# Float64 weight correction moved from VectorE to GpSimd, two early loads issued by ScalarE, and a new written order

## The chip, the cores and the metric

One core of one Trainium2 chip runs the whole program. The metric is device time in microseconds (us), the median of three runs. One more run was taken with the hardware profiler; its own time and its span are given below. TensorE (PE) does matmuls and its weight loads (PEld), VectorE is DVE, ScalarE is ACT, GpSimd is POOL, and SyncE (SP) issues DMAs.

## The reference

Attention with 8 batches, 8 heads, 576 positions and head size 64, in which every query keeps only its 32 highest scores, and behind it a SoLU block on 4608 tokens:

```
scores = q @ k.T / sqrt(64)
kth    = the 32nd largest score of each row
attn   = softmax(scores where scores >= kth) @ v
x      = attn as (4608, 512)
h      = x @ w_in                       # w_in (512, 1024), float64
solu   = h * softmax(h)
ln     = (solu - mean) / sqrt(var + 1e-6) * g_ln
out    = ln @ w_out                     # w_out (1024, 512), float64
```

q, k, v and g_ln are float32; w_in and w_out arrive as float64 and are carried as 64-bit words.

## The kernel before

The work is cut into 32 steps (four a batch). A step takes four chunks of 128 queries, two heads each, and one tail chunk, so it has nine blocks of 128 rows by 576 scores, numbered j = 0 to 8. For each step:

- `scores` (L1869) makes the scores on PE in seven units, `evac` (L1892) copies each to the tile X on ACT.
- `estimate`, `length`, `root`, `gained` (L1815 to L1853) work out a first threshold per row; `root` and `gained` are small GpSimd operations.
- `count0` (L1920) counts the scores over it, per block j, on DVE for the first blocks (line L1907) and on ACT for the last three or four (L1915). `second`, `moved`, `even` (L1923 to L1938) form a better threshold, `count1` (L1947) counts again on ACT and leaves the signs in `sg`.
- `side`, `nearest`, `best` (L1955 to L1984) and the steps behind them find the exact 32nd score on DVE from the values nearest to the threshold; `keep` (L2052, line L2055) masks the exponentials E on DVE.
- `transpose_p` and `copy_p` turn E into PT, `attn_v` and `attn_t` multiply it with V on PE, `copy_v` (L2236 to L2249) scales the result on DVE into xTm and xTt. The scales go through DRAM: `turn_r`, `copy_r`, `rd_out`, `rd_in` (L2098 to L2121).

36 blocks of 128 tokens follow as their inputs come ready: `mm1` (L2260), `hexp`, `solu` (L2279), `square`, `spread`, `ln` (L2302, on GpSimd), `transpose_ln`, `copy_ln`, `mm2` (L2324), `store`, `send`.

The weights come in 16 chunks of 128 x 512 64-bit words, in about the first 140 us. For each chunk `load_w` (L1570) brings the raw words, `w_bits` (L1590) forms a float32 from the high words in two DVE operations (L1594, L1598), and `w_corr` (L1603) forms the correction from the low words in two more: L1606 masks out the power of two, L1610 multiplies the low word, 2^-52 and that power. `w_sum` (L1614) adds value and correction on PE by identity matmuls (L1617, L1618), and `w_copy` (L1622) brings the sum into w_in or w_out on ACT. At the end of the kernel the words are loaded again (`w_again`), and `w_exp` (DVE, L1635) and `w_check` (ACT) check their exponents.

`load_k` (L1664) and `load_t` (L1675) bring a head pair's main keys and its 64-row tails; the tails of all pairs go into one tile, `qk_tails`, so the tails of pair n + 1 may be written only after PE has read those of pair n (`prep_k`, L1736). `key_stats` (L1772) of both head pairs of a step come ahead of its `estimate`.

All engines but SP run in an order written out by hand: `PLACES` (L490) holds one number for each piece of work, `arranged` (L472) sorts by it, and the pieces are emitted in that order. Each engine works its own instructions in that order and waits at each for what it needs; SP's DMA issues follow it too. The numbers have no other effect than this order.

Of the kernel before, what the change touches and what calls it, by code (L numbers as in the profile page):

```python
# [465 lines left out]
WIDE_KINDS = ("w_bits", "w_corr", "w_sum", "w_copy", "w_again", "w_exp", "w_check")  # L466
# [5 lines left out]
def arranged(w_wide):  # L472
# [11 lines left out]
    if not w_wide:  # L484
# [10 lines left out]
    ],  # L495
    "load_t": [
# [3 lines left out]
    ],  # L500
    "load_v": [
# [3 lines left out]
    ],  # L505
    "prep_k": [
# [3 lines left out]
    ],  # L510
    "prep_tc": [
# [3 lines left out]
    ],  # L515
    "prep_kc": [
# [3 lines left out]
    ],  # L520
    "key_square": [
# [3 lines left out]
    ],  # L525
    "tail_square": [
# [3 lines left out]
    ],  # L530
    "key_stats": [
# [3 lines left out]
    ],  # L535
    "load_q": [
# [3 lines left out]
    ],  # L540
    "prep_q": [
# [3 lines left out]
    ],  # L545
    "prep_qc": [
# [3 lines left out]
    ],  # L550
    "query_square": [
# [3 lines left out]
    ],  # L555
    "estimate": [
# [3 lines left out]
    ],  # L560
    "length": [
# [3 lines left out]
    ],  # L565
    "root": [
# [3 lines left out]
    ],  # L570
    "gained": [
# [3 lines left out]
    ],  # L575
    "scores": [
        [11258, 12553, 17516, 19137, 11903, 18161, 7601],
        [34101, 29755, 38452, 39097, 26637, 41622, 27493],
        [60356, 61001, 70269, 68119, 59706, 69587, 55581],
        [99604, 94705, 91454, 100249, 94055, 92764, 86988],  # L580
        [130314, 129600, 144747, 140254, 128950, 139466, 131165],
        [173269, 170744, 166391, 165746, 172587, 164928, 161517],
        [204423, 203718, 194005, 195300, 196330, 194650, 201137],
        [231483, 232773, 232128, 229768, 234330, 230833, 235843],
        [251834, 266825, 267507, 265859, 254298, 265209, 247223],
        [284259, 289097, 283545, 288452, 282895, 284941, 286789],
# [820 lines left out]
def fast_path(  # L1407
# [179 lines left out]
    def words(n, k):  # L1587
        return w_raw[n].bitcast(U32).rearrange("p (f w) -> p f w", w=2)[:, :, k]
# [850 lines left out]
```

## Time and profile before

| what | before |
|---|---|
| median of 3 runs | 1107.89 us (1107.51 to 1108.54) |
| the profiled execution: own time | 1107.34 us |
| the profiled execution: span from first to last instruction | 1105.4 us |
| DVE busy | 1005.6 us, 91% |
| PE busy (its ends are modelled) | 1044.7 us, 95% |
| ACT busy | 999.2 us, 90% |
| POOL busy | 241.0 us, 22% |

The chain of waits follows the work that ended last back to the start; the windows give each engine's busy time in a stretch; the rows of lines give a group's busy time, its mean duration in ns, and how long its engine sat idle before it and for whom. A timeline row is start, duration, engine, line, operation, tiles and count, with the idle time before it in brackets.

### The profile page before, as it was taken

The page shows a single profiled execution, that of the slowest core. Times are in us where ns is not written, and L with a number is a line of the kernel's source. Part 1 is how long each engine was busy: PE and PEld are TensorE (multiplying, and loading weights), DVE is VectorE, ACT ScalarE, POOL GpSimd, SP SyncE. Part 2 cuts the span into 40 slices and gives each one's busy share as a digit, 9 for nine tenths or more (in the row PEclk, how much of TensorE's full clock was granted, in tenths as well). Part 3 has the DMA queues.
Part 4 walks back from the last instruction along what each step waited for, and adds up shares of the span by engine and source line. Part 5 has one row for each costly group of instructions (what it writes and reads, how often), then busy time and mean ns, then how long its engine had stood idle before and what let it go on. Part 6 is the DMA issues. An engine that isn't in the chain of part 4 may idle for free.

```text
span 1105.4 us, 22954 instructions
## 1 busy us (share of the span) xinstructions
PE 1044.7 (95%) x7980; PEld 583.2 (53%) x7980; DVE 1005.6 (91%) x2929; ACT 999.2 (90%) x1976; POOL 241.0 (22%) x401
## 2 busy tenths in 40 slices
PE   5778898999999999999999999999999999999996
PEld 3355454554555555555555556555555555555543
DVE  5999999999999999999999898999999989998720
ACT  7999798999999989999998998999999999999632
POOL 1202221303233112222214013212213122220110
PEclk9679899999999999999999999999999999999998
DMA  8312211121121112121121202210211111123411
GB/s 221 112 44 79 79 42 52 34 55 27 48 63 44 53 34 65 31 55 54 47 61 42 53 22 74 55 34 30 67 53 32 44 33 47 49 76 109 155 40 32
DMA packets 110425, 64.81 MB, mean 59 GB/s; under 512 B 89422, under 2 KB 97883, under 8 KB 110299
## 3 DMA queue, kind: packets, MB, share of 16 engines
q1 hardware_dynamic: 110298, 63.25, 20.5%
q8 instruction: 65, 1.06, 0.4%
q14 instruction: 62, 0.50, 0.1%
HBM read 53.65 MB, written 9.57 MB: 57 GB/s over the span
## 4 chain that ended last, share of the span: by engine, by line
DVE 44%; PE 25%; ACT 19%; issue 4%; DMA 1%; POOL 0%; SPq 0%; DVEq 0%; ACTq 0%
DVE w L1971 10%; DVE w L1982 10%; DVE E L2055 8%; PE o_ps L2324 8%; PE h_ps L2260 7%; DVE junkv L1907 5%; ACT sg L1950 5%; ACT X L1902 4%; PE s_ps L1887 3%; DVE solu L2279 3%; ACT PT L2156 2%; ACT E L2007 2%; PE om L2207 2%; DVE by L1999 2%; PE tp_p L1701 2%
## 5 line engine op out<-in xcount | busy, mean ns | idle before, releaser
L2324 PE MATMUL o_ps<-w_out,lnT 128*128 128x512 f32 x576 | 261.1, 599 | 0.9 <-DVE xTt L2249 0.8
L2260 PE MATMUL h_ps<-w_in,xTm 128*128 128x512 f32 x512 | 230.3, 598 | 3.4 <-DVE xTm L2242 2.9
L1982 DVE MAX8 w<-w 128x8 f32<-128x288 f32 x576 | 224.6, 445 | 0.1
L1950 ACT ACTIVATE sg<-X,t 128x576 int8<-128x576 f32 x256 | 198.2, 790 | 7.6 <-DVE t L1935 6.7
L1971 DVE SCALAR_TENSOR_TENSOR w<-X,al,sg 128x576 f32<-128x576 f32 x256 | 202.9, 814 | 0.5
L2055 DVE SCALAR_TENSOR_TENSOR E<-X,kth,E 128x576 f32<-128x576 f32 x256 | 200.2, 821 | 1.3
L2324 PEld LDWEIGHTS o_ps<-w_out,lnT 128*128 128x128 f32 x576 | 105.2, 190 | 119.0 <-issue 113.4
L1887 PE MATMUL s_ps<-kT,qT 64*128 64x192 f32 (+1 forms) x1024 | 155.2, 437 | 12.4 <-ACT kT L1721 4.9
L1907 DVE TENSOR_SCALAR_CACHE_REDUCE junkv<-X,t 128x576 uint8<-128x576 f32 x188 | 146.0, 805 | 8.1 <-ACT X L1902 7.1
L1902 ACT ACTIVATE X<-s_ps 128x768 f32<-128x768 f32 x192 | 146.0, 837 | 7.2 <-PE s_ps L1887 6.9
L2260 PEld LDWEIGHTS h_ps<-w_in,xTm 128*128 128x128 f32 x512 | 94.1, 190 | 110.4 <-issue 102.2
L2007 ACT ACTIVATE E<-X 128x1152 f32<-128x1152 f32 x128 | 150.7, 1201 | 0.0
L2156 ACT COPY PT<-tp_p 128x1024 f32<-128x1024 f32 x128 | 131.7, 1040 | 11.3 <-PE tp_p L1701 8.9
L2207 PE MATMUL om<-PT,vm 128*64 128x256 f32 (+1 forms) x1024 | 135.6, 410 | 2.6 <-ACT PT L2190 1.5
L1887 PEld LDWEIGHTS s_ps<-kT,qT 64*128 64x128 f32 x1024 | 90.9, 197 | 53.8 <-ACT X L1902 7.0
L1842 POOL TENSOR_TENSOR zs<-zs,phalf 128x9 f32<-128x9 f32 x32 | 63.8, 1994 | 173.0 <-DVE zs L1834 138.5
L1701 PE MATMUL tp_p<-ident,E 64*128 64x64 f32 x2048 | 87.8, 229 | 13.0 <-DVE E L2055 8.0
L2207 PEld LDWEIGHTS om<-PT,vm 128*64 128x64 f32 x1024 | 68.9, 137 | 55.2 <-issue 4.0
L1701 PEld LDWEIGHTS tp_p<-ident,E 64*128 64x128 f32 x2048 | 76.4, 142 | 36.2 <-issue 13.3
L1943 POOL TENSOR_SCALAR tt<-t 128x9 f32<-128x9 f32 x32 | 12.9, 403 | 273.0 <-DVE t L1935 239.8
L2295 POOL TENSOR_SCALAR var<-var 128x1 f32<-128x1 f32 x36 | 11.0, 307 | 225.6 <-ACT e_sb L2289 225.2
L2271 ACT ACTIVATE e_sb<-h_ps 128x1024 f32<-128x1024 f32 x36 | 37.5, 1042 | 21.0 <-PE h_ps L2260 21.0
(150 smaller groups left out, 1567.2 us busy)
## 6 DMA issues: line engine op xcount, KB each, us to landing
km<-in_k_dram SPq DMA_DIRECT2D x32, 256.0 KB
q_sb<-in_q_dram SPq DMA_DIRECT2D x64, 128.0 KB
vm<-in_v_dram SPq DMA_DIRECT2D x32, 256.0 KB
out_dram<-osb SPq DMA_DIRECT2D x32, 256.0 KB
scales<-rows SPq DMA_DIRECT2D x58, 128.0 KB
w_raw<-in_moe_w_in_dram SPq DMA_DIRECT2D x8, 512.0 KB
w_raw<-in_moe_w_out_dram SPq DMA_DIRECT2D x8, 512.0 KB
w_again<-in_moe_w_in_dram SPq DMA_DIRECT2D x8, 512.0 KB
```

The source lines that it names most:

```text
L1701: nc.tensor.transpose(out[:, a, :], part(rows), ident[rows, rows])
L1887: nc.tensor.matmul(out=s[:, n, m * part : (m + 1) * part], lhsT=queries_of(i, t)[hd, :], rhs=kT[hd, k0 : k0 + part], start=True, stop=True,)
L1902: nc.scalar.activation(out=x, in_=s, func=AF.Copy, scale=scale)
L1907: nc.vector.tensor_scalar(out=junk, in0=x_of(i, j), scalar1=st[i][t][:, j : j + 1], scalar2=None, op0=ALU.is_ge, op1=ALU.add, accum_out=co ...
L1950: nc.scalar.activation(out=d["sg", j], in_=x_of(i, j), func=AF.Sign, scale=-(1.0 + 2.0**-23), bias=d["t1"][:, j : j + 1], accum_out=column ...
L1971: nc.vector.scalar_tensor_tensor(out=w, in0=x_of(i, j), scalar=d["al"][:, j : j + 1], in1=d.pop(("sg", j)), op0=ALU.subtract, op1=ALU.mult,)
L1982: nc.vector.max(w8[:, j, 8 * half : 8 * half + 8], w[:, half * SH : (half + 1) * SH])
L2007: nc.scalar.activation(out=d["E", t][:, 0 : x2_of(i, t).shape[1]], in_=x2_of(i, t), func=AF.Exp)
L2055: nc.vector.scalar_tensor_tensor(out=e, in0=x_of(i, j), scalar=d["kth"][:, j : j + 1], in1=e, op0=ALU.is_ge, op1=ALU.mult, accum_out=den_a ...
L2207: nc.tensor.matmul(out=o[h * D : (h + 1) * D, cols], lhsT=vm[:, h, c, :], rhs=pt[:, h * NM + c, :], start=(c == 0), stop=False,)
L2260: nc.tensor.matmul(out=h[:, half, :], lhsT=x[:, c, :], rhs=w_in[:, c, half * 512 : (half + 1) * 512], start=(c == 0), stop=(c == NP - 1),)
L2324: nc.tensor.matmul(out=o, lhsT=d["lnT"][:, c, :], rhs=w_out[:, c, :], start=(c == 0), stop=(c == NF - 1),)
```

## The change

1. The second operation of `w_corr` (L1610, DVE) goes. In its place come two GpSimd operations for each chunk: `w_low` turns the low words into float32, times 2^-52, in place, and `w_prod` multiplies them with the power of two. `w_sum` now follows `w_prod`.
2. The three DMAs of `load_t` for pairs 0 and 1 are issued by ACT; those of the other 30 pairs stay with SP.
3. Every place in `PLACES` is a new number, so the order of all pieces on all engines is another one. No piece other than those of 1 is added or left out.

The core of the diff (the places of the other kinds change in the same way):

```diff
-WIDE_KINDS = ("w_bits", "w_corr", "w_sum", "w_copy", "w_again", "w_exp", "w_check")
+WIDE_KINDS = ("w_bits", "w_corr", "w_low", "w_prod", "w_sum", "w_copy", "w_again", "w_exp", "w_check")
...
     "load_t": [
-        0, 10470, 16060, 26190, 37940, 65560, 72482, 102319, 123769, 206223, 214502, 236530, 245024,
...
+        0, 4608, 15310, 25880, 33290, 67285, 78694, 91724, 101724, 195521, 214555, 219213, 231656,
...
     "w_corr": [
-        8667, 13577, 19167, 25147, 28047, 43000, 51790, 61625, 81592, 84152, 97994, 117104, 112195,
-        124205, 131589, 136794,
+        6862, 14072, 19568, 22993, 30672, 35893, 59932, 64324, 71269, 80062, 90454, 96808, 107484,
+        109456, 123803, 132050,
+    ],
+    "w_low": [
+        7192, 14456, 18783, 24773, 29150, 36223, 57745, 62981, 69080, 79245, 89124, 95021, 105950,
+        114239, 124941, 130783,
+    ],
+    "w_prod": [
+        8047, 16116, 20093, 25628, 32452, 39405, 60457, 65379, 73124, 88114, 91577, 97863, 111601,
+        115706, 126841, 133105,
     ],
...
             op0=ALU.bitwise_and,
         )
-        nc.vector.scalar_tensor_tensor(
-            out=corr, in0=words(n, 0), scalar=2.0**-52, in1=corr, op0=ALU.mult, op1=ALU.mult
-        )
+
+    def w_low(n):
+
+        nc.gpsimd.tensor_scalar(
+            out=words(n, 0).bitcast(F32), in0=words(n, 0), scalar1=2.0**-52, scalar2=1.0,
+            op0=ALU.mult, op1=ALU.mult,
+        )
+
+    def w_prod(n):
+
+        corr = w_tmp[n][:, 1, :]
+        nc.gpsimd.tensor_tensor(out=corr, in0=words(n, 0).bitcast(F32), in1=corr, op=ALU.mult)
...
     def load_t(n):
         b, hp = pairs[n]
         hh = slice(2 * hp, 2 * hp + 2)
+        queue = nc.scalar if n < 2 else nc.sync
         for h in range(2):
             hd = slice(h * ST, (h + 1) * ST)
-            nc.sync.dma_start(out=qk_tails[hd, 0, hd], in_=q[b, 2 * hp + h, SM:S, :])
-        nc.sync.dma_start(
+            queue.dma_start(out=qk_tails[hd, 0, hd], in_=q[b, 2 * hp + h, SM:S, :])
+        queue.dma_start(
```

What the new order holds, counted in the sorted lists: the pieces between one step's `second` and the next one's, for the steps from 17 on.

```
interval ending at second(i), i =   17 18 19 20 21 22 23 24 25 26 27 28 29 30 31
scores units, before                 9  5  7  7  9  8  4  7 12  2  7  7  7  7  7
scores units, after                  7  7  7  7  7  7  7  8  6  7  7  7  7  7  7
transpose_p, before                  5  0  5  6  4  5  2  5  6  0  6  4  4  4  7
transpose_p, after                   4  2  6  4  3  5  4  4  4  4  2  5  4  5  6
keep, before                        11  2 12  9 15  7  2 15 12  0 14  9 13  3 15
keep, after                         10  8 14  8  6 12  5 14  4 10  8  9  9  9 18
```

Up to the interval of step 16 both orders hold seven units in each interval. Before the first `count0` of step 0, DVE has three chunks' `w_bits` and `w_corr` in the order before and two in the order after. On ACT, three `evac`, two `exps` and one `w_copy` that stand ahead of `prep_kc` and `key_square` of pair 1 in the order before stand behind them in the order after. Behind the last `keep` of step 31 stand eight `w_exp` in the order before and five in the order after, and the first half of `mm2` of token block 32 now stands on PE just ahead of `turn_r`; otherwise PE's list from there to the end holds the same pieces.

## Rows read from the trace of the kernel before

**Rows 1.** Page, part 1: busy time of each engine, share of the span, instructions.
```profile
PE 1044.7 (95%) x7980; PEld 583.2 (53%) x7980; DVE 1005.6 (91%) x2929; ACT 999.2 (90%) x1976; POOL 241.0 (22%) x401
```
**Rows 2.** Page, part 4: the chain that ended last, share by engine.
```profile
DVE 44%; PE 25%; ACT 19%; issue 4%; DMA 1%; POOL 0%; SPq 0%; DVEq 0%; ACTq 0%
```
**Rows 3.** Windows: stretch, length, busy us and instructions of PE, PEld, DVE, ACT, POOL.
```profile
0.00:30.00 30.00, 17.37 (x115) 10.38 (x116) 16.76 (x46) 23.15 (x54) 5.33 (x43) 0.91 0.82 214
30.00:200.00 170.00, 144.99 (x1081) 82.05 (x1081) 165.00 (x468) 151.79 (x310) 33.16 (x51) 0.88 0.23 64
200.00:600.00 400.00, 393.90 (x3128) 221.91 (x3130) 394.53 (x1159) 388.85 (x775) 104.28 (x149) 1.00 0.18 47
600.00:700.00 100.00, 99.75 (x827) 57.31 (x824) 91.88 (x272) 94.10 (x180) 20.97 (x34) 1.00 0.21 56
700.00:900.00 200.00, 196.72 (x1551) 110.38 (x1549) 195.13 (x571) 192.32 (x382) 43.98 (x71) 1.00 0.16 43
900.00:1020.00 120.00, 118.11 (x910) 65.32 (x908) 111.28 (x321) 114.56 (x219) 22.98 (x39) 1.00 0.22 67
1020.00:1041.00 21.00, 19.90 (x176) 11.03 (x172) 20.69 (x64) 13.19 (x22) 4.53 (x6) 1.00 0.26 81
1041.00:1105.50 64.50, 54.02 (x226) 24.78 (x222) 10.31 (x37) 21.23 (x41) 5.79 (x9) 0.95 0.21 71
```
**Rows 4.** Waits of DVE from 30 to 1045 us: total us, times, longest.
```profile
DVE al L1959 <- ACT sg L1950: 8.3, 9, 2.6
DVE junkv L1907 <- ACT X L1902: 7.1, 7, 2.3
```
**Rows 5.** Timeline of PE late in the kernel, and its group of lines.
```profile
L2324 PE MATMUL o_ps<-w_out,lnT 128*128 128x512 f32 x576 | 261.1, 599 | 0.9 <-DVE xTt L2249 0.8
...
1070.84 3.60 PE L2324 MATMUL o_ps<-w_out,lnT 128*128 128x512 f32 x8
```
**Rows 6.** Lines of DVE: busy us, mean ns of one, idle before.
```profile
L1610 DVE SCALAR_TENSOR_TENSOR w_tmp<-w_raw,w_tmp 128x512 f32<-128x512 uint32 x16 | 11.1, 693 | 0.5
...
L1635 DVE TENSOR_SCALAR w_exp<-w_again 128x512 uint32<-128x512 uint32 x16 | 6.6, 418 | 0.5 <-DMA w_again<-in_moe_w_out_dram 0.4
```
**Rows 7.** Lines and timeline: GpSimd's ln, alone and beside DVE's L1971.
```profile
L2302 POOL TENSOR_SCALAR solu<-solu,nmu,rstd 128x1024 f32<-128x1024 f32 x36 | 52.6, 1461 | 2.7
...
271.65 2.48 POOL L2302 TENSOR_SCALAR solu<-solu,nmu,rstd 128x1024 f32<-128x1024 f32 x1
...
271.61 1.53 DVE L1971 SCALAR_TENSOR_TENSOR w<-X,al,sg 128x576 f32<-128x576 f32 x2
...
1072.39 1.20 POOL L2302 TENSOR_SCALAR solu<-solu,nmu,rstd 128x1024 f32<-128x1024 f32 x1
```
**Rows 8.** Timeline of the head: tails' loads, first transposes, second statistics, first count.
```profile
1.54 1.32 SPq L1680 DMA_DIRECT2D qk_tails<-in_q_dram  x2
...
4.54 0.88 PE L1701 MATMUL tp_k<-ident,qk_tails 64*128 64x64 f32 x3 [4.54 <-DMA qk_tails<-in_q_dram]
...
7.96 1.14 SPq L1680 DMA_DIRECT2D qk_tails<-in_q_dram  x2
...
17.13 0.17 DVE L1775 TENSOR_TENSOR stats<-sums,heads 128x6 bf16<-128x6 f32 x1 [3.06 <-ACT junka L1760]
...
20.73 0.81 DVE L1907 TENSOR_SCALAR_CACHE_REDUCE junkv<-X,t 128x576 uint8<-128x576 f32 x1
```
**Rows 9.** Timeline of DVE: three of its longer waits after 600 us.
```profile
686.45 0.81 DVE L1907 TENSOR_SCALAR_CACHE_REDUCE junkv<-X,t 128x576 uint8<-128x576 f32 x1 [2.31 <-ACT X L1902]
...
909.90 0.16 DVE L1959 SCALAR_TENSOR_TENSOR al<-n,tt 128x3 f32<-128x3 f32 x1 [2.59 <-ACT sg L1950]
...
1011.83 0.16 DVE L1959 SCALAR_TENSOR_TENSOR al<-n,tt 128x3 f32<-128x3 f32 x1 [2.31 <-ACT sg L1950]
```
**Rows 10.** Timeline of DVE: the last keep, and the first work behind it that waits.
```profile
1040.08 0.81 DVE L2055 SCALAR_TENSOR_TENSOR E<-X,kth,E 128x576 f32<-128x576 f32 x1
...
1052.99 0.42 DVE L2242 TENSOR_TENSOR xTm<-om,scales 128x256 f32<-128x256 f32 x1 [9.44 <-DMA scales<-rows]
```

More of the change, by code (lines that the diff above doesn't have):

```diff
@@ new lines @@
+        [418590, 422749, 424404],
+        [452470, 450937, 445478],
+        [477483, 481195, 482713],
+        [505619, 516227, 511076],
+        [545047, 549481, 536746],
+        [564045, 562089, 557252],
+        [601445, 610894, 606233],
+        [643774, 634569, 637711],
+        [672761, 661316, 667592],
+        [703135, 696636, 700755],
+        [727715, 724003, 731412],
+        [759304, 756889, 765270],
+        [787034, 790733, 783309],
+        [822109, 820397, 814205],
+        [848274, 855359, 840877],
@@ new lines @@
+        [275108, 285359],
+        [305449, 305883],
+        [342206, 347449],
+        [370873, 376052],
+        [390631, 400502],
+        [429461, 422421],
+        [457046, 456922],
+        [483828, 479154],
+        [510983, 526282],
+        [541356, 574329],
+        [581133, 594733],
+        [610272, 622309],
+        [642613, 647265],
+        [669277, 681514],
+        [707340, 712474],
+        [723112, 740238],
+        [763699, 774869],
+        [792960, 799382],
+        [829587, 840506],
@@ L1112 @@
-        [1026055, 1024041],
+        [54788, 56731],
+        [86178, 96392],
+        [132116, 121257],
+        [161139, 153396],
+        [188898, 200924],
+        [227288, 225994],
+        [244648, 242500],
+        [280606, 285906],
+        [308109, 309511],
+        [344219, 350235],
+        [371736, 377034],
+        [393321, 401987],
+        [430842, 423036],
+        [458616, 457306],
+        [485060, 481832],
+        [514166, 526673],
+        [551059, 579023],
+        [581827, 595573],
@@ L1113 @@
+        [612000, 622770],
+        [644939, 648033],
+        [676025, 684516],
+        [709801, 718583],
+        [728282, 741554],
+        [766692, 775349],
+        [795173, 799855],
+        [836821, 841177],
+        [862460, 869152],
+        [893255, 883843],
+        [914013, 925937],
+        [944496, 949092],
+        [973617, 984528],
+        [1003660, 1003226],
     ],
     "attn_v": [
-        [75477, 80408],
-        [102152, 96541],
-        [147218, 152075],
-        [177266, 174067],
@@ new lines @@
+        [379898, 382102],
+        [409138, 411342],
+        [444994, 447198],
+        [467404, 465448],
+        [503773, 501995],
+        [531375, 533579],
+        [574627, 592032],
+        [604720, 606924],
+        [632843, 635047],
+        [660696, 662900],
+        [690830, 689048],
+        [717425, 719629],
+        [744888, 751386],
+        [776098, 778889],
+        [824352, 830630],
+        [854864, 857068],
+        [878348, 880552],
+        [899044, 901248],
+        [926782, 928986],
@@ L1147 @@
+        [961242, 965949],
+        [984112, 987038],
+        [1005787, 1004009],
     ],
     "attn_t": [
[L1149 to L1163 removed]
@@ new lines @@
+        [138041, 145323],
+        [170322, 169895],
+        [222428, 217936],
+        [232966, 232539],
+        [260671, 263036],
+        [290487, 291021],
+        [337677, 338211],
+        [366823, 367357],
+        [383880, 384414],
+        [413594, 414128],
+        [448976, 449510],
+        [470035, 469608],
+        [506404, 505977],
+        [535357, 535891],
+        [576884, 593863],
+        [608702, 609236],
+        [636825, 637359],
+        [665158, 664731],
+        [693461, 693034],
@@ L1209 @@
-        [903052, 902720],
-        [930671, 931133],
-        [957593, 968345],
-        [985616, 986078],
-        [1013854, 1013522],
-        [1034742, 1035204],
+        [65379, 75503],
+        [94826, 101494],
+        [142570, 146360],
+        [171614, 170697],
+        [223558, 218870],
+        [235158, 234726],
+        [262887, 263772],
+        [292157, 291825],
+        [338694, 339156],
+        [368121, 368583],
+        [388723, 389185],
+        [418658, 415298],
+        [450143, 450605],
@@ new lines @@
+        [470871, 470449],
+        [510614, 510282],
+        [536814, 537276],
+        [578410, 595200],
+        [610100, 610562],
+        [637779, 638241],
+        [666270, 665938],
+        [696173, 696704],
+        [722801, 722469],
+        [749605, 756477],
+        [780295, 781497],
+        [827995, 837022],
+        [859791, 860253],
+        [884159, 883100],
+        [903850, 904312],
+        [933822, 948215],
+        [964655, 968525],
+        [989640, 990902],
+        [1011467, 1011929],
@@ L1271 @@
-        [1042750, 1046185],
-        [1050539, 1057409],
+        [105772, 102337],
+        [109314, 113919],
+        [175773, 172338],
+        [184448, 187883],
+        [235882, 239721],
+        [243918, 249835],
+        [293056, 297763],
+        [309622, 306187],
+        [317764, 314329],
+        [376350, 372008],
+        [391496, 385617],
+        [433497, 430062],
+        [437041, 440476],
+        [471675, 484429],
+        [497729, 494294],
+        [541957, 545392],
+        [553232, 549797],
@@ new lines @@
+        [561565, 556776],
+        [611765, 615309],
+        [627716, 624281],
+        [669878, 673313],
+        [681812, 677718],
+        [723713, 727148],
+        [735487, 740529],
+        [782419, 785854],
+        [799673, 793832],
+        [804380, 808928],
+        [862009, 866351],
+        [874191, 870756],
+        [910494, 907059],
+        [931465, 934900],
+        [972852, 969417],
+        [979831, 976396],
+        [1012554, 1015989],
+        [1019531, 1022966],
+        [1027177, 1030612],
@@ L1348 @@
-        [1010972, 1015263],
-        [1018805, 1025501],
-        [1053974, 1061700],
-        [1065242, 1069533],
-        [1073075, 1076617],
+        [131150, 139178],
+        [155067, 159719],
+        [195368, 199703],
+        [203247, 208000],
+        [263630, 268035],
+        [275778, 279322],
+        [321199, 325251],
+        [342807, 347740],
+        [352206, 356611],
+        [396458, 400800],
+        [415331, 418873],
+        [453374, 458150],
+        [475110, 479445],
+        [507105, 511832],
@@ new lines @@
+        [522734, 527572],
+        [565000, 569955],
+        [577585, 582726],
+        [596403, 599947],
+        [638810, 643717],
+        [652756, 656539],
+        [694162, 698876],
+        [708926, 713268],
+        [753811, 757353],
+        [764300, 771321],
+        [812363, 815905],
+        [833416, 836958],
+        [842171, 845715],
+        [890592, 894136],
+        [914899, 921757],
+        [938335, 942980],
+        [950510, 954293],
+        [989944, 993486],
+        [999185, 1009119],
@@ L2386, in fast_path @@
         copy_v, mm1, hexp, solu, square, spread, ln, transpose_ln, copy_ln, mm2, store, send, load_g, turn_g,
-        copy_g, load_w, w_bits, w_corr, w_sum, w_copy, w_gain, w_again, w_exp, w_check, w_passed,
+        copy_g, load_w, w_bits, w_corr, w_low, w_prod, w_sum, w_copy, w_gain, w_again, w_exp, w_check, w_passed,
         w_verdict,
```

728 lines of the change are left out of this document (269 added, 459 removed), and 588 rows, old and new, of the table PLACES.

## Prediction

> **What bounds the kernel now.** I read part 1 of the page first, then the chain, then the windows, then the waits of the engine that the chain names. Part 1 has three engines at 90% or more and GpSimd at 22% [rows 1]; PE looks the fullest. The chain says otherwise: 44% of it is DVE, 25% PE, 19% ACT [rows 2]. The windows say where: DVE sits idle for 13.2 of the first 30 us, then for 5.0 in 30 to 200, 5.5 in 200 to 600, 8.1 in 600 to 700, 4.9 in 700 to 900, 8.7 in 900 to 1020 and 0.3 up to 1041 [rows 3]. So from 30 to 1041 us it works 97% of the time, and its list sets the pace up to the last `keep`, which ends at 1040.9 [rows 10]. What is left of idle time there are mostly waits for ACT: 8.3 us for the signs and 7.1 us for X [rows 4]. Behind the last `keep` comes a tail of 64.5 us, in which DVE has 10.3 us of work and PE 54.0 [rows 3].
>
> PE's 95% is not a bound of the same kind. A 512-column matmul is listed at 599 ns, yet eight in a row take 3.60 us, 0.45 each [rows 5]; the recorded busy time holds overlap and queueing. The Trainium skill, Trainium Kernel Development and Optimization, section Performance Expectations, calls matmul busy time a bad metric because matmuls are pipelined. By that rule the trace agrees, and it lowers the chance of the third rival below.
>
> The end is therefore: DVE's idle time in the head, plus its work up to the last `keep`, plus its waits in the middle, plus the tail. I go through these four, against the profiled execution's own 1107.34 us; 1.9 us of it lie around the span, and the median of the runs stands 0.55 above it.
>
> **DVE's work.** Sixteen L1610 operations of 693 ns go, 11.1 us [rows 6], all in the first 140 us and in a stretch where DVE is 97% busy. Since everything behind stands in DVE's list, all of it moves up: -11.1. The other three operations of a chunk stay. Three more `w_exp` of 418 ns now stand ahead of the last `keep` [rows 6]: +1.3. The two GpSimd operations cost DVE nothing as far as the trace shows: beside a GpSimd operation of 2.48 us two L1971 of 576 columns took 1.53 us [rows 7], no more for a column than L1610's 693 ns for 512 [rows 6].
>
> **The GpSimd operations.** The trace has none of this size. The nearest is `ln`, a one-input operation on 1024 columns: 1.20 us alone, 1.46 on average, 2.48 beside L1971 [rows 7]. For 512 columns `w_low` lies between half the lowest, 0.6, and the highest, 2.48; I take 0.75, near half the mean. `w_prod` reads two tensors; I put it between 0.6 and 2.48 and take 1.2, above half the mean since it reads twice. `w_low` runs beside what is left of `w_corr`, so `w_sum` comes 1.2 - 0.69 = 0.5 us later for each chunk. Behind `w_sum` on PE stand scores and transposes, and behind those `evac` and `count0`. What covers it: PE has 25.0 us idle in 30 to 200 and 12.6 in the first 30 [rows 3], and 16 x 0.5 = 8 us go into that. I charge +0.5; without the cover it would be +8, and at the highest durations it is the last rival. GpSimd itself has room: 16 x 1.95 = 31 us beside 38.5 us that it is busy in the first 200 [rows 3]. `root` now stands behind such pieces in its list; a step's first count could start a us or two late, which I keep in the range.
>
> The trace shows the shared cost in the other direction: the same `ln` takes twice as long beside an operation of DVE that reads two tensors [rows 7]. The Trainium skill, GPSIMD Engine Reference, section 1 (Specifications), says the SBUF interfaces are shared with VectorE, with contention when DVE reads two SBUF inputs; the trace agrees, 1.20 against 2.48 us. Its section 3 (Performance versus the Vector engine) speaks against this change: GpSimd is called the wrong choice for ordinary elementwise work, and a two-input operation is put at about 2.6 cycles an element at 1.2 GHz. From that an estimate for `w_prod` is 1.1 us without start-up; the sum by it would not differ by more than 0.1.
>
> **The head.** SP issues the tails of pair 0 from 1.54 us on and those of pair 1 from 7.96 on [rows 8]; on ACT the second set can go out as soon as PE has read the first, which ends near 4.54 + 0.88 = 5.4, some 2.5 us sooner. The second statistics come at 17.13 and the first count at 20.73 [rows 8]. In the new order ACT also turns to pair 1 before three copies, two `exps` and a `w_copy`, so the first count should start four to five us earlier. But that is not four us of gain: one chunk of some 2.2 us (an estimate: two operations like each of [rows 6], 2 x 0.69 + 2 x 0.42) is done after it instead of before. Up to the count DVE has three chunks of work now, 6.7 us and under 2 us of small pieces, so it idles some 12 of the 20.73 us; with two chunks, and the count near 16, it idles some 11. ACT pays three issues of 0.66 us, half of 1.32 [rows 8], ahead of its first copies. I take -1.0, between -4 (all of the earlier start) and +3 (ACT's wait for PE and its issues delay the first keys, and the count stays where it was).
>
> **The middle.** This is where I chose most. In the even part, 200 to 600 us, DVE idles 1.4 us per 100 [rows 3]. In 600 to 700 and 900 to 1020 it idles 16.8 us in 220, where that rate would give 3.0: an excess of 13.8. The order before is uneven there. Between the `second` of steps 17 and 18 it has five scores units and no transpose, later nine, eight, four, twelve and two units, and from 0 to 15 `keep`; the wait at 686.45 lies in an interval with nine units, that at 909.90 in one with 13 `keep` [rows 9]. The new order has seven units in nearly every interval and 4 to 14 `keep` in those of the same steps. Where ACT is handed its work evenly, I expect the even rate. One place stays uneven: 18 `keep` stand ahead of `second` of the last step (15 before), so I keep the 2.3 us wait at 1011.83, just behind that `second` [rows 9]. That makes -11.5. The bounds are wide: +5 (ACT and PE, which have less room when all else is 20 us shorter, make DVE wait as much as before and a little more) and -20 (nearly all waits go).
>
> **The tail.** The pieces behind the last `keep` are the same, but half a `mm2`, 3.6 us [rows 5], now stands ahead of `turn_r`. It starts while the last `keep` still runs and ends after it; of its length I count 1.5 against the path that goes through the scales' trip to DRAM, which DVE waits 9.44 us for [rows 10]. Fewer `w_exp` behind it change nothing, DVE is idle there. +1.5, between 0 and +3.
>
> **Sum.** -11.1 + 1.3 + 0.5 - 1.0 - 11.5 + 1.5 = -20.3 us, so 1107.34 - 20.3 = 1087.0 for a profiled execution, and 1087.6 for the median.
>
> **Rivals.**
> 1. Only the removed work counts. The waits of the middle stay in size and change place, because ACT, at 90% [rows 1], is as full as before. The waits for ACT speak for it [rows 4]; that they cluster where the order is uneven speaks against it. -20.3 + 11.5 = -8.8: 1099.1.
> 2. More comes: of the 27.2 us idle in 200 to 1020 [rows 3], 15.7 in the forecast, only 10 stay, and the first count keeps more of its lead. -20.3 - 5.7 - 3 = -29.0: 1078.9. For it: 0.3 us idle in 1020 to 1041, so DVE can run without waits. Against it: even the long even part idles 1.4 per 100 us, which is 11 for those 820 us.
> 3. PE is the bound after all and takes back what DVE gives: no change, 1108. For it: 393.9 of 400 us busy [rows 3]. Against it: the 0.45 us above, and a chain with 44% DVE.
> 4. Slower. GpSimd's two operations take 2.48 us each, since DVE reads two tensors for most of the time. Then 4.96 us stand where 0.43 + 0.69 stood, each `w_sum` is 3.8 us late, and what queues behind it on PE with it: 16 x 3.8 = 61 us, of which the 37.6 us of PE's idle time before 200 us take up their part. 61 - 37.6 = 24 late, less the gain of 20.3: 1111. It decides from (37.6 + 20.3) / 16 = 3.6 us a chunk on. Against it: 2.48 is a worst case for twice the columns.
>
> **How the numbers follow.** The forecast 0.55, rivals 1 to 4 with 0.21, 0.11, 0.05 and 0.08. The forecast's own range is 1081 to 1093. To leave out 2 in 10, the range reaches to rival 2 and past rival 1: 1079 to 1101. Within 0.2% (2.2 us, about what a measurement of this kernel tells from no change) is rival 3; slower is rival 4. Faster 0.87, same 0.05, slower 0.08.
>
> **What would show it.** In the changed kernel's windows DVE's busy total is 11 us lower, and the last `keep` ends near 1019. `w_prod` is near 1.2 us, and PE's waits for it at L1617 and L1618 sum to under 8 us. The first count starts near 16 us. DVE's waits for X and the signs fall from 15.4 to about 5 us, with none over 1 us in 600 to 700. From the last `keep` to the end stay 64 to 67 us. The prediction is wrong in its main step if the waits of the middle come back elsewhere (time near 1099), and in its cover if waits for `w_prod` exceed 15 us before 150 us.

## The result, and the profile after

The changed kernel takes 1093.41 us (median of 4 runs, 1092.84 to 1094.46) where the kernel before takes 1108.22 (1107.51 to 1109.45, run beside it): a ratio of 0.9866 with a 95% interval of 0.9849 to 0.9883. It is 14.8 us faster, where 20.3 were forecast; the forecast for the median was 1087.6. The profiled execution has a time of its own of 1093.13 us and a span of 1091.3.

First part 1 and the chain of the page of the kernel after, which answer to [rows 1, 2]:

```profile
PE 1037.9 (95%) x7980; PEld 582.7 (53%) x7980; DVE 1001.0 (92%) x2913; ACT 998.4 (91%) x1976; POOL 284.5 (26%) x433
...
PE 51%; DVE 28%; ACT 15%; issue 3%; DMA 1%; POOL 1%; SPq 0%; DVEq 0%; ACTq 0%
```

Sixteen operations fewer stand on DVE, 11.1 us of work by [rows 6], yet its busy time fell by 4.6 us only. The chain now follows PE for half of its length, as it does for 40 to 53% in every kernel below with the new order and for 23 to 27% in those with the old one. The windows of the kernel after, in the columns of [rows 3], say where the time went:

```profile
0.00:30.00 30.00, 15.86 (x92) 9.33 (x94) 12.85 (x35) 17.91 (x41) 11.38 (x50) 0.97 0.76 189
30.00:200.00 170.00, 143.83 (x1110) 82.83 (x1106) 166.81 (x462) 156.13 (x323) 68.90 (x79) 0.87 0.25 69
200.00:600.00 400.00, 396.36 (x3147) 222.74 (x3147) 395.52 (x1164) 393.57 (x780) 101.33 (x147) 1.00 0.18 48
600.00:700.00 100.00, 99.91 (x834) 57.83 (x831) 95.71 (x281) 95.67 (x186) 21.63 (x35) 1.00 0.20 54
700.00:900.00 200.00, 198.22 (x1563) 112.05 (x1562) 196.96 (x583) 197.36 (x397) 45.22 (x70) 1.00 0.17 45
900.00:1003.00 103.00, 103.00 (x831) 58.43 (x830) 98.82 (x289) 98.45 (x185) 25.50 (x36) 1.00 0.24 76
1003.00:1026.60 23.60, 23.33 (x179) 12.69 (x178) 23.03 (x65) 18.01 (x32) 4.79 (x8) 1.00 0.38 114
1026.60:1091.30 64.70, 57.36 (x241) 26.81 (x241) 11.28 (x41) 21.32 (x39) 5.80 (x9) 0.96 0.17 55
```

The third pair is DVE. It idles 17.15 us of the first 30 (13.2 before), 3.2 up to 200 (5.0), 4.5 up to 600 (5.5), 4.3 in 600 to 700 (8.1), 3.0 up to 900 (4.9) and 4.2 in the 103 us up to 1003. The last `keep` ends at 1028.6 where it ended at 1040.9. I cut both traces at 30 us, at 200 us and at the end of the last `keep`, and count DVE's idle time in each part, its busy time up to the last `keep`, and the rest:

```
                                 before    after   measured   forecast
DVE busy, up to the last keep     995.2    991.7     -3.5       -9.8
DVE idle, 0 to 30                  13.2     17.1     +3.9       -1.0
DVE idle, 30 to 200                 5.0      3.2     -1.8       +0.5
DVE idle, 200 to the last keep     27.5     16.6    -10.9      -11.5
last keep to the end of the span   64.6     62.8     -1.8       +1.5
sum                                                 -14.1      -20.3
```

### The profile page after: what moved, and what is told of

Same layout as the page of the kernel before. It is cut to its first block, busy times and chain, and to the rows that moved or that the text cites. A ratio compares the mean times of both kernels' runs of the same rounds, so it can differ in the third digit from the quotient of the medians.

```text
span 1091.3 us, 22980 instructions
## 1 busy us (share of the span) xinstructions
PE 1037.9 (95%) x7980; PEld 582.7 (53%) x7980; DVE 1001.0 (92%) x2913; ACT 998.4 (91%) x1976; POOL 284.5 (26%) x433
## 4 chain that ended last, share of the span: by engine, by line
PE 51%; DVE 28%; ACT 15%; issue 3%; DMA 1%; POOL 1%; SPq 0%; DVEq 0%; ACTq 0%
PE o_ps L2342 15%; PE h_ps L2278 13%; PE s_ps L1905 6%; DVE w L1989 6%; PE om L2225 6%; DVE w L2000 6%; DVE E L2073 5%; ACT sg L1968 4%; DVE junkv L1925 4%; PE tp_p L1719 4%; ACT X L1920 2%; ACT E L2025 2%; ACT PT L2174 2%; DVE solu L2297 2%; PE s_ps L1894 2%
## 5 line engine op out<-in xcount | busy, mean ns | idle before, releaser
L2073 DVE SCALAR_TENSOR_TENSOR E<-X,kth,E 128x576 f32<-128x576 f32 x256 | 204.0, 829 | 2.0 <-ACT E L2025 1.4
L1989 DVE SCALAR_TENSOR_TENSOR w<-X,al,sg 128x576 f32<-128x576 f32 x256 | 205.1, 824 | 0.1
L1905 PE MATMUL s_ps<-kT,qT 64*128 64x192 f32 (+1 forms) x1024 | 149.5, 430 | 4.3 <-DVE solu L2297 1.7
L1925 DVE TENSOR_SCALAR_CACHE_REDUCE junkv<-X,t 128x576 uint8<-128x576 f32 x188 | 148.5, 804 | 5.1 <-ACT X L1920 4.0
L1860 POOL TENSOR_TENSOR zs<-zs,phalf 128x9 f32<-128x9 f32 x32 | 68.7, 2146 | 161.6 <-DVE zs L1852 148.4
L1961 POOL TENSOR_SCALAR tt<-t 128x9 f32<-128x9 f32 x32 | 16.2, 508 | 250.6 <-DVE t L1953 208.8
L2313 POOL TENSOR_SCALAR var<-var 128x1 f32<-128x1 f32 x36 | 13.9, 387 | 196.7 <-ACT e_sb L2307 196.4
L2320 POOL TENSOR_SCALAR solu<-solu,nmu,rstd 128x1024 f32<-128x1024 f32 x36 | 53.6, 1490 | 3.3
```

The costliest lines, as they stand in the source:

```text
L1905: nc.tensor.matmul(out=s[:, n, m * part : (m + 1) * part], lhsT=queries_of(i, t)[hd, :], rhs=kT[hd, k0 : k0 + part], start=True, stop=True,)
L1925: nc.vector.tensor_scalar(out=junk, in0=x_of(i, j), scalar1=st[i][t][:, j : j + 1], scalar2=None, op0=ALU.is_ge, op1=ALU.add, accum_out=co ...
L1989: nc.vector.scalar_tensor_tensor(out=w, in0=x_of(i, j), scalar=d["al"][:, j : j + 1], in1=d.pop(("sg", j)), op0=ALU.subtract, op1=ALU.mult,)
L2073: nc.vector.scalar_tensor_tensor(out=e, in0=x_of(i, j), scalar=d["kth"][:, j : j + 1], in1=e, op0=ALU.is_ge, op1=ALU.mult, accum_out=den_a ...
```

## The experiments

The medians below are of four to twelve timed runs, but for one kernel with a single run; the ratio is to the kernel before, run beside it on the same chip (medians of 1108.3 to 1109.3 us), with its 95% interval. Kernels that ran on different chips are best compared by these ratios. "Held" is counted in the trace in this way: an operation of DVE that ends over 150 ns later behind its forerunner than the median of its kind does, beside a running GpSimd operation; the excess over the median is the held time. DVE's counts are left out: some of them show 0.16 to 0.18 us also where GpSimd rests.

### What each part of the change is worth

**Order alone.** The changed kernel, with the low words multiplied on DVE again and all tails loaded by SP:

```diff
+        nc.vector.scalar_tensor_tensor(
+            out=corr, in0=words(n, 0), scalar=2.0**-52, in1=corr, op0=ALU.mult, op1=ALU.mult
+        )
...
     def w_low(n):
-        nc.gpsimd.tensor_scalar(...)
+        pass
     def w_prod(n):
-        nc.gpsimd.tensor_tensor(...)
+        pass
...
-        queue = nc.scalar if n < 2 else nc.sync
+        queue = nc.sync
```

> The new order with the old work: the low words are multiplied by VectorE again, in one operation behind the mask at w_corr's places, and all tails are loaded by SyncE at their new places. Theory A (the gain is the order's; the move to GpSimd is worth about nothing because GpSimd's operations hold VectorE's; the loads by ScalarE cost about 4 us in the head): VectorE gets 11.1 us back and loses 10.4 us of holds, the head regains 4: about 1090 us. Theory B (the move is worth its 11 us, and the order lost it elsewhere): 1093.4 + 11 - 4 = about 1100 us. If SyncE's tails of pair 1, which now stand ahead of the second keys, hold back the loads behind them, both are some us later, and the first count shows it.

Measured: 1092.40 us, ratio 0.9848 (0.9835 to 0.986). The order alone makes the whole gain, as theory A had it. The window of this kernel from 200 us on:

```profile
200.00:1020.00 820.00, 813.98 (x6468) 459.67 (x6464) 802.80 (x2357) 799.11 (x1569) 198.33 (x296) 1.00 0.19 53
```

DVE idles 17.2 us from 200 to the last `keep`, as in the kernel after (16.6). Its whole busy time is 1001.5 us with the sixteen operations in it, against 1001.0 in the kernel after without them.

**The move undone, the loads kept on ACT.** The first two hunks of the diff above, without the third.

> The changed kernel with one part undone: the low words are multiplied by VectorE again, in one operation behind the mask, in the new order and with ScalarE's loads of the first tails kept. Theory A (the move to GpSimd is worth about nothing, since holds give back what VectorE saves): 1092 to 1095 us, beside 1093.4 for the changed kernel. Theory B (the move gains at least a few us in the order that was made for it): over 1097 us.

Measured: 1094.14 us, 0.9863 (0.9845 to 0.988); DVE busy 1001.1 us, idle 17.3 us from 200 to the last `keep`. Beside the kernel after (1093.41 us, 0.9866) the move to GpSimd is worth -0.7 us, or +0.3 by the ratios. The kernel with all tails on SP, shown below, gives a second pair that differs in the move alone, both run on the same chip: 1092.96 us with the low words on GpSimd, 1092.40 with them on DVE, +0.6. In the new order the move can't be told from nothing.

**The move alone, in the old order.** The kernel before with `w_low` and `w_prod` on GpSimd, placed right behind their `w_corr`:

```diff
+    "w_low": [8668, 13578, 19168, 25148, ...
+    "w_prod": [8669, 13579, 19169, 25149, ...
...
-        nc.vector.scalar_tensor_tensor(...)
+    def w_low(n):
+        nc.gpsimd.tensor_scalar(...)
+    def w_prod(n):
+        nc.gpsimd.tensor_tensor(...)
```

> The kernel before, its order and its loads, with the low words on GpSimd: w_low and w_prod directly behind w_corr. Theory A (holds give back what VectorE saves): VectorE loses 11.1 us of its own work and gains 8 to 12 us of holds: 1106 to 1109 us. Theory B (the move is worth its 11 us): 1097 to 1099 us. A third reading (TensorE waits for GpSimd at w_sum): over 1110 us.

Measured: 1112.98 us, 1.0034 (1.0023 to 1.0045): some 4 us slower. Its window from 200 us on:

```profile
200.00:1020.00 820.00, 808.01 (x6406) 454.96 (x6405) 792.94 (x2323) 789.72 (x1551) 191.13 (x292) 1.00 0.18 50
```

And two lines of its timeline:

```profile
104.08 2.59 DVE L1982 SCALAR_TENSOR_TENSOR w<-X,al,sg 128x576 f32<-128x576 f32 x2
104.33 1.72 POOL L1623 TENSOR_TENSOR w_tmp<-w_raw,w_tmp 128x512 f32<-128x512 f32 x1 [5.30 <-DVE w_tmp L1608]
```

DVE's idle time from 200 on is 27.5 us, as before: the middle belongs to the order. The pair of `w` operations took 2.59 us beside `w_prod`, 1.53 in [rows 7]. Over the kernel `w_prod` held 12 of DVE's operations for 11.9 us and `w_low` 11 for 4.0: 15.9 us lost against 11.1 saved. The time is that of the third reading, PE waiting for `w_prod`, but the cause is not: PE does wait 6.0 us for it between 20 and 160 us, yet of the 4.9 us that the span is longer, 4.6 are DVE's busy time up to the last `keep`, and its idle time up to 200 us grew by 0.7 only.

**The loads, by themselves.** The changed kernel with the tails of pairs 0 and 1 on SP (third hunk above), and the kernel before with them on ACT (`queue = nc.scalar if n < 2 else nc.sync`, as in the change):

> The changed kernel with the tails of pairs 0 and 1 issued by SyncE again, at the same places; nothing else differs. Theory A (the issue by ScalarE delays the head: the tails land late beside the first weights, and ScalarE's table load waits behind the issues): first count 4 to 5 us sooner than the 21.7 of the changed kernel, about 1089.5 us. Theory B (the head is limited by what lands, whoever issues it): first count within 1 us and 1093 to 1095 us.

> The kernel before with the tails of pairs 0 and 1 issued by ScalarE, at the places before. Theory A (the issue by ScalarE delays ScalarE's first work in any order, but a lead of 3 us in the first count is lost again by 190 us): first ScalarE operation at 10 us or later instead of 5.9, first count 2 to 4 us later than 20.7, and the time the same within 2 us, 1107 to 1111 us. Theory B (the delay in the head is of the new order alone): first count within 1 us of 20.7 and the time that of before.

Measured: 1092.96 us, 0.9852 (0.9839 to 0.9864) with SP; 1109.45 us, 1.0006 (0.9997 to 1.0015) for ACT in the old order. By total time the loads make no difference that can be told: going by the ratios, their issue by ACT costs 1.6 us in the kernel after, 1.7 in the new order with the low words on DVE and 0.7 in the old order, always the same way, but with intervals that overlap. Their delay in the head is real: the first count starts at 18.1 us with SP and 21.7 with ACT in the new order, 20.7 and 23.3 in the old one. Where the new order's SP kernel loses its lead, the windows show; first this kernel, then the kernel after:

```profile
125.00:140.00 15.00, 11.82 (x91) 7.53 (x90) 12.72 (x35) 9.48 (x14) 9.72 (x13) 0.77 0.19 54
...
170.00:190.00 20.00, 20.00 (x168) 11.96 (x165) 17.64 (x53) 15.43 (x23) 0.00 (x0) 0.91 0.16 45
```

```profile
125.00:140.00 15.00, 11.81 (x69) 5.97 (x69) 14.83 (x45) 10.37 (x23) 6.67 (x8) 0.92 0.31 89
...
170.00:190.00 20.00, 20.00 (x194) 12.07 (x192) 20.00 (x59) 16.61 (x27) 1.14 (x2) 1.00 0.17 47
```

The lead of 3.5 us, measured at the `second` of a step, holds until step 3 and is gone at step 5. In these stretches DVE idles 4.6 us where the kernel after idles 0.2, waiting for X, and PE's granted clock is 0.77 and 0.91 on average where the kernel after has 0.92 and 1.00. Whether the clock is the cause was not settled. Over the first 200 us DVE idles the same in both: 14.0 + 6.3 us with SP, 17.1 + 3.2 with ACT.

### What the GpSimd operations cost

**No low words at all.** The changed kernel without `w_low` and `w_prod`, the correction masked to zero (the low words are left out of the weights):

```diff
-            out=corr.bitcast(U32), in0=val.bitcast(U32), scalar1=0xFF800000, scalar2=None,
+            out=corr.bitcast(U32), in0=val.bitcast(U32), scalar1=0x0, scalar2=None,
```

with both bodies replaced by `pass`.

> The changed kernel without w_low and w_prod, and no operation in their place: the correction is masked to zero, so the low words of the weights are left out. Theory A (holds cost VectorE about 10 us on the path): 1093.4 - 10 = about 1083 us, VectorE's held operations before 140 us gone. Theory B (the held time would have been waiting time anyway, VectorE waits for ScalarE or TensorE instead): 1091 to 1094 us.

Measured: 1087.46 us, 0.9806 (0.9792 to 0.982), 5.9 us below the kernel after (6.6 by the ratios), between the two theories. DVE's busy time up to the last `keep` is 981.5 us, 10.1 below, though DVE itself does the very same list. The windows:

```profile
0.00:30.00 30.00, 17.23 (x108) 9.93 (x108) 11.87 (x38) 18.98 (x45) 4.83 (x43) 0.94 0.77 194
30.00:200.00 170.00, 146.32 (x1147) 84.86 (x1146) 163.56 (x474) 159.97 (x329) 37.46 (x56) 0.88 0.24 68
```

GpSimd is down from 68.90 to 37.46 us in 30 to 200, and DVE gets through 474 operations where the kernel after gets through 462. Of the 10.1 us, 4.7 come back as idle time: 1.0 more up to 30 us, 3.3 more in 30 to 200, 0.4 behind.

**The same work in small pieces.** `w_low` in two pieces of 256 columns, `w_prod` in four of 128, so that a hold would be short:

```diff
+        for c in range(4):
+            cols = slice(c * 128, (c + 1) * 128)
+            corr = w_tmp[n][:, 1, cols]
+            nc.gpsimd.tensor_tensor(
+                out=corr, in0=words(n, 0)[:, cols].bitcast(F32), in1=corr, op=ALU.mult
+            )
```

> The changed kernel with w_low cut into two operations of 256 columns and w_prod into four of 128; the arithmetic and the places are the same. Theory A (an operation of VectorE that reads two tensors waits for the end of the GpSimd operation that is running, whatever its length): the held time by w_low and w_prod falls from 10.4 us to 2 to 4, and the time to between that of the run without low words (1087.5) and the changed kernel (1093.4): about 1089 us. Theory B (VectorE is slowed in proportion to GpSimd's work, so every piece holds again): held time stays at 9 to 11 us, 1093 to 1096 us.

Measured: 1091.73 us, 0.9854 (0.9839 to 0.987). DVE busy up to the last `keep` 988.8 us, 2.8 below; the holds of the low words are 28 for 6.5 us, none over 0.31 us, where they were 15 for 10.4. Its line of `w_prod`:

```profile
L1633 POOL TENSOR_TENSOR w_tmp<-w_raw,w_tmp 128x128 f32<-128x128 f32 x64 | 36.5, 601 | 23.4 <-DVE w_tmp L1614 20.9 <-PE tp_k L1725 1.6 <-DVE t L1955 0.7
```

And two pieces of its timeline, the first undisturbed by DVE:

```profile
8.66 1.72 POOL L1633 TENSOR_TENSOR w_tmp<-w_raw,w_tmp 128x128 f32<-128x128 f32 x4 [0.44 <-DVE w_tmp L1614]
...
92.92 3.85 POOL L1633 TENSOR_TENSOR w_tmp<-w_raw,w_tmp 128x128 f32<-128x128 f32 x4
93.57 1.01 DVE L2079 SCALAR_TENSOR_TENSOR E<-X,kth,E 128x576 f32<-128x576 f32 x1
94.50 1.00 DVE L2079 SCALAR_TENSOR_TENSOR E<-X,kth,E 128x576 f32<-128x576 f32 x1
```

In the kernel after, the first `w_prod`, whole and undisturbed as well, is

```profile
8.78 1.29 POOL L1629 TENSOR_TENSOR w_tmp<-w_raw,w_tmp 128x512 f32<-128x512 f32 x1 [1.15 <-DVE w_tmp L1614]
```

Beside the four pieces of 92.92 each `keep` takes 1.0 us where it takes 0.81 undisturbed: the two engines take turns. The price is on GpSimd, 36.5 us where 24.6 were: four pieces take 1.72 us undisturbed where one whole takes 1.29, and the rest is waiting for DVE. The time fell by 1.7 us (1.3 by the ratios), with intervals that overlap.

**`ln` in four pieces**, 256 columns each, in the changed kernel, by the same means.

> The changed kernel with ln, the GpSimd operation on 1024 columns of each token block, cut into four of 256; everything else as changed. It holds VectorE for 8.1 us in 13 places in the changed kernel (4.8 us in 7 places before). Theory A (holds end with the GpSimd operation, and they lie on VectorE's path): held time by ln under 3 us, and 4 to 6 us off: about 1088 us. Theory B (held time is waiting time in any case, or the pieces hold as often): 1092 to 1096 us.

Measured: 1095.69 us, 0.9882 (0.9868 to 0.9896): 2.3 us above the kernel after, as theory B had it. The holds by `ln` fell from 8.0 to about 6 us, but its 144 pieces take

```profile
L2322 POOL TENSOR_SCALAR solu<-solu,nmu,rstd 128x256 f32<-128x256 f32 x144 | 110.8, 781 | 3.2
...
1061.33 2.16 POOL L2322 TENSOR_SCALAR solu<-solu,nmu,rstd 128x256 f32<-128x256 f32 x4
```

110.8 us, where 36 whole ones take 53.6. Undisturbed, at 1061.33, four pieces take 2.16 us where one whole `ln` takes 1.20 [rows 7]: 36 times that difference is 35 of the 57 us, and the rest is waiting. Cutting an operation shortens each hold, but buys it with GpSimd time.

### The head

**Table first.** An activation of one column ahead of ACT's loads, in the changed kernel (a single run):

```diff
+    warm = const.tile([P, 1], F32, tag="warm", name="warm")
+    nc.scalar.activation(out=warm, in_=phalf, func=AF.Exp)
```

> The changed kernel with one small activation of one column ahead of all of ScalarE's work, so that the load of its table, 1.28 us, comes before the issues of the tails and not behind them. Theory A (the table load behind the issues is part of the delay): ScalarE's first copy at about 10 us instead of 11.2, and the first count 1 us sooner than 21.7. Theory B (the late tails alone set it, their landing at 7.0 and 7.8 us): the tails of pair 0 go out 1.2 us later and the first copy comes no sooner than 11.2. The whole time within 2 us of 1093 in both.

Measured: 1091.37 us; the table load starts at 0.72 us, the first copy at 8.57 where it was 11.21, and the first count at 19.9. Its lead over the kernel after, 1.8 us at the `second` of step 0, is still 1.8 at that of step 31. The same edit on the kernel with the low words on DVE, and on the one with small pieces:

> The new order with the low words on VectorE, ScalarE's loads kept, and the early table load: the same test of the head without GpSimd's operations. Theory A (the table's 1.8 us is kept): 1.5 to 2 us below the run with the move undone. Theory B (the lead is lost): the same time as it.

> A version meant to beat the changed kernel: w_low in two and w_prod in four pieces, and the small activation ahead of ScalarE's loads that brings the table load forward. Theory A (both effects are separate: holds of 10.4 us fell to 6.5 for about 1.7 us of time, the earlier table gave 1.8 us): 1089 to 1090.5 us. Theory B (a lead from the head is lost again by 190 us, as with the tails by SyncE): 1091 to 1092 us.

Measured: 1091.93 us, 0.9843 (0.9827 to 0.9858) and 1089.13 us, 0.9825 (0.9806 to 0.9844). Each is 2.0 to 2.6 us below its partner without the edit (1093.41, 1094.14, 1091.73). Where both of a pair have intervals they overlap, and the first was run once, but all three go the same way. The last one, quarters and table, is the fastest kernel that computes the whole reference: its interval lies below that of the changed kernel, 0.9849 to 0.9883.

## Why the prediction came out as it did

**The middle: right in size, and shown to be the order's.** Waits from 200 us on fell by 10.9 us, 11.5 forecast. The three kernels with the old order have 27.4 or 27.5 us there, every kernel with the new one 16.5 to 17.5, whatever multiplies the low words and whoever loads. So the order did it. That its evenness did it is argued and not tested, and the count of units alone doesn't tell where the waits stood: in the trace of before the waits for X and the signs between the `second` of step 16 and that of step 31 sum to 11.9 us, of which 4.9 lie in the four intervals with more than seven units, 6.9 in the eight with just seven and 0.1 in the three with fewer. In the kernel after they sum to 2.0. The waits for the signs and X from 30 to 1030 us, which answer to [rows 4]:

```profile
DVE junkv L1925 <- ACT X L1920: 3.2, 6, 1.3
...
DVE al L1977 <- ACT sg L1968: 2.7, 4, 1.9
```

They sum to 5.9 where about 5 were forecast. The wait that I kept, for the signs just behind the `second` of the last step, is still there, 1.9 us for the 2.3 that were kept:

```profile
997.50 0.16 DVE L1977 SCALAR_TENSOR_TENSOR al<-n,tt 128x3 f32<-128x3 f32 x1 [1.87 <-ACT sg L1968]
```

Rival 1, in which the waits only change place, falls on this, though its 1099 us lay no farther from the result than the forecast. The mark for 600 to 700 held: the one wait of over 1 us that is left there, 1.15 us, is for the exponentials E and not for X or the signs. Rival 2 falls as well, 16.6 us of waits stay where it left 10. Rival 3, PE as the bound that takes everything back, falls by the time; with a chain that now follows PE for half of its length, PE bounds more of the kernel than it did, and by how much no experiment took apart.

**DVE's work: the step that failed.** "The two GpSimd operations cost DVE nothing as far as the trace shows" is wrong. They hold DVE's operations. The clearest place in the timeline of the kernel after:

```profile
27.81 1.56 DVE L1602 TENSOR_SCALAR w_tmp<-w_raw 128x512 uint32<-128x512 uint32 x1
...
27.79 1.29 POOL L1629 TENSOR_TENSOR w_tmp<-w_raw,w_tmp 128x512 f32<-128x512 f32 x1 [2.55 <-DVE t L1949]
```

An operation that takes 0.42 us undisturbed (L1594 of before, the same operation) starts 0.02 us behind `w_prod` and takes 1.56: it ends 0.29 us behind `w_prod`'s end. A little later both directions stand in a row:

```profile
95.63 0.81 DVE L2073 SCALAR_TENSOR_TENSOR E<-X,kth,E 128x576 f32<-128x576 f32 x1
95.73 1.88 POOL L1629 TENSOR_TENSOR w_tmp<-w_raw,w_tmp 128x512 f32<-128x512 f32 x1
96.37 1.85 DVE L2073 SCALAR_TENSOR_TENSOR E<-X,kth,E 128x576 f32<-128x576 f32 x1
97.69 1.04 POOL L1621 TENSOR_SCALAR w_raw<-w_raw 128x512 f32<-128x512 uint32 x1
98.15 1.18 DVE L2073 SCALAR_TENSOR_TENSOR E<-X,kth,E 128x576 f32<-128x576 f32 x1
```

The `keep` of 95.63 was first and keeps its 0.81 us; `w_prod`, 0.10 us behind it, takes 1.88 instead of 1.29; the next `keep` starts while `w_prod` runs and takes 1.85. Here whoever starts first goes on, and the other waits for its end. In [rows 7] stands such a wait too, and I misread it: there two DVE operations in a row, the first 0.04 us ahead of `ln`, were the ones that went on and `ln` waited, and I took DVE to be immune. The trace of before had the other case too, six times, 4.6 us in all, always beside `ln`; here the first:

```profile
128.36 1.86 POOL L2302 TENSOR_SCALAR solu<-solu,nmu,rstd 128x1024 f32<-128x1024 f32 x1
...
129.24 1.58 DVE L2055 SCALAR_TENSOR_TENSOR E<-X,kth,E 128x576 f32<-128x576 f32 x1
```

Three of these six are such operations of `keep`, whose mean of 821 ns over 256 hid them. With `ln` the recorded start does not always decide. Eleven of its 36 operations in the kernel after take 1.87 us or more, and in each of these, as in [rows 7], a two-input operation of DVE that started behind `ln` was not held, so that `ln` waited for it as well. Here the second of the two operations starts 0.58 us behind `ln` and goes ahead of it:

```profile
905.64 2.37 POOL L2320 TENSOR_SCALAR solu<-solu,nmu,rstd 128x1024 f32<-128x1024 f32 x1
...
905.50 1.53 DVE L1989 SCALAR_TENSOR_TENSOR w<-X,al,sg 128x576 f32<-128x576 f32 x2
```

The Trainium skill, SBUF — State Buffer, section SBUF: two separate sides, has the rule: VectorE and GpSimd share a pair of ports as an exclusive lock, held for a whole instruction by whichever of a GpSimd operation and a VectorE operation of certain kinds (two SBUF inputs, or a two-port mode) starts first. By that rule the rows of `w_prod` agree, and the eleven `ln` don't by their recorded starts; why is open. Held in the kernel after were 24 operations with two inputs and four TENSOR_SCALAR, for 1.13 us at most. Whether those four ran in a two-port mode no run shows. None of the 41 MAX8 was held that started with at least 0.3 us of `w_low`, `w_prod` or `ln` still to run.

In the kernel after `w_prod` holds 9 operations for 8.0 us, `w_low` 6 for 2.4, and `ln` 13 for 8.0 (4.6 before). So DVE's busy time of -4.6 us splits as: -11.1 for the operations taken away, +10.4 for the holds by the two new ones, +3.4 for more holds by `ln`, which stands elsewhere in the new order; the remaining -7.3 is what is left over. In the order-only kernel the same comparison (1005.6 to 1001.5 us, 3.0 more held by `ln`) leaves -7.1, so it comes from the order too; it lies in many small operations that follow sooner on their forerunners (the 32 operations that form `zk_all` add 7.5 us to the busy time where they added 8.5). No experiment took that apart. It is also where luck came in: 13.8 us of holds that the forecast did not have were half made up for by 7 us that it did not have either. Taking the low words away altogether gives back 5.9 of the 10.4 us, and the old order, where more operations are caught, turns the move into a loss: both show the holds to be the price.

The other half of the step, that all of the 11.1 us move up, was too high as well. The kernel without low words lies 6.7 us below the one with the sixteen operations back on DVE (1087.46 and 1094.14; 6.3 by the ratios), and DVE idles 5.0 us more in it. So even without any hold the move would have been worth some 6 us in the new order, not 11.

**GpSimd's durations: nearly right, and the wrong question.** Lines of GpSimd in the kernel after:

```profile
L1629 POOL TENSOR_TENSOR w_tmp<-w_raw,w_tmp 128x512 f32<-128x512 f32 x16 | 24.6, 1540 | 32.3 <-DVE w_tmp L1614 24.3 <-PE s_ps L1905 5.0 <-DVE t L1949 2.6
L1621 POOL TENSOR_SCALAR w_raw<-w_raw 128x512 f32<-128x512 uint32 x16 | 13.3, 831 | 9.3 <-DMA w_raw<-in_moe_w_in_dram 8.1
```

And from its waits of PE, 20 to 160 us (total us, times, longest):

```profile
PE w_tp L1635 <- POOL w_tmp L1629: 4.6, 3, 1.7
```

They take 1.54 and 0.83 us, with 1.2 and 0.75 forecast; undisturbed it is 1.29 and 0.65, and the rest is waiting for DVE. PE waits 4.6 us for `w_prod`, forecast under 8, and DVE's idle time of 30 to 200 fell rather than rose. The cover held, and rival 4, a late `w_sum`, did not come. A slower kernel did come in the old order, by the holds and not by that wait.

**The head: wrong in sign.** Forecast was a first count near 16 us; it came at 21.72. In the timeline of the kernel after:

```profile
1.19 1.25 ACTq L1698 DMA_DIRECT2D qk_tails<-in_q_dram  x2
4.64 0.33 PE L1719 MATMUL tp_k<-ident,qk_tails 64*128 64x64 f32 x1 [4.64 <-DMA qk_tails<-in_q_dram]
7.01 0.37 PE L1719 MATMUL tp_k<-ident,qk_tails 64*128 64x64 f32 x1 [2.03 <-DMA qk_tails<-in_q_dram]
7.86 1.29 ACTq L1698 DMA_DIRECT2D qk_tails<-in_q_dram  x2
9.91 1.28 ACT L1771 ACT_TABLE_LOAD   x1 [9.91 <-DMA qk_tails<-in_q_dram]
11.21 0.60 ACT L1771 ACTIVATE kT<-tp_k 128x512 f32<-128x512 f32 x1
21.72 0.81 DVE L1925 TENSOR_SCALAR_CACHE_REDUCE junkv<-X,t 128x576 uint8<-128x576 f32 x1 [0.82 <-ACT X L1920]
```

Two things were left out of the sum. The tails of pair 0 came in one after the other, at 4.64 and 7.01 for PE, where all stood ready at 4.54 in [rows 8]; so the second set could go out at 7.86 and not at 5.4. And ACT issues in order: its table load, and with it its first copy, waits behind the second set, 11.21 where the first operation of ACT ran at 5.9 before. That is not all of the miss: with the loads on SP DVE idles 14.0 us of the first 30 and the first count comes at 18.1, still 0.8 us more than before where 1.0 less was forecast. So 3.1 of the 4.9 us are the issues by ACT; the rest was not taken apart. The bound of +3 for this term was named, "ACT's wait for PE and its issues", and the measured +3.9 lies past it. What it cost the total is some 2 us by the three kernels with the table first, and 0.7 to 1.7 by the three pairs that move the loads alone, which can't be told from nothing; between these the size stays open.

**The tail.** Forecast +1.5, measured -1.8. The half `mm2` ahead of `turn_r` costs nothing that shows; `xTm` starts 10.3 us behind the last `keep`, 12.1 before:

```profile
1027.76 0.80 DVE L2073 SCALAR_TENSOR_TENSOR E<-X,kth,E 128x576 f32<-128x576 f32 x1
...
1038.89 0.42 DVE L2260 TENSOR_TENSOR xTm<-om,scales 128x256 f32<-128x256 f32 x1 [8.74 <-DMA scales<-rows]
```

No experiment looked at it by itself, but it goes with the order: every kernel with the new one has 62.6 to 63.1 us there, the three with the old one, the kernel before among them, 64.1 to 65.2.

Together: the DVE term missed by 6.3 us and the head by 4.9, the middle by 0.6; the stretch from 30 to 200 gave 2.3 more than forecast and the tail 3.3. That is the 6.2 us between -20.3 and -14.1. Of the other marks, DVE's busy total fell by 4.6 us instead of 11, the last `keep` ended at 1028.6 instead of 1019, and the tail of 62.8 us lies below the 64 to 67.

## What to carry to other kernels

An operation moved from DVE to GpSimd is not off DVE: where DVE's list is full of two-input operations, count for each moved one what it will hold there, and look for it operation by operation, since a group's mean hides three long ones in 256. Nor does all of the work that leaves a busy engine's list come off the time: of 11.1 us some 6 did here, in the kernel without low words. The order in which the engines work was worth more here than the work that was moved: setting the idle rate of the uneven stretches to that of the even one gave that term within 1 us, and the order alone made the whole gain. A DMA issue put on an engine that also computes brings all that stands behind it in line behind the DMA's own waits, a table load included.

## What was not expected of the hardware

- A GpSimd operation has a large fixed part: undisturbed, `w_prod` in four pieces of 128 columns takes 1.72 us and whole 1.29, `ln` in four pieces of 256 columns 2.16 us and whole 1.20.
- DVE's operation can be held even when GpSimd starts only 0.02 us sooner, and then until GpSimd's end; its recorded time holds the wait, so the engine looks busy while it stands still. The recorded start alone does not say which of the two will wait: eleven `ln` waited for an operation of DVE that started behind them.
